# Reading the streamed operands of both feed-forward products from the last column to the first

## The chip, the cores and the metric

The kernel runs on one core of a Trainium2 chip. The metric is the device time of one execution in microseconds, of which the median of several runs is compared. Five engines matter: TensorE (PE in the profile, with its weight loads as PEld), VectorE (DVE), ScalarE (ACT), GpSimd (POOL) and SyncE (SP), whose queue carries the DMA transfers.

## The reference

The reference first runs a recurrence over 768 tokens for 4 batches of 8 heads of 48 channels, and then a feed-forward layer over all 3072 tokens, all in float32:

```python
for t in range(S):
    ar, ai = a_re_n[:, :, t, :, None], a_im_n[:, :, t, :, None]
    new_re = ar * S_re - ai * S_im
    new_im = ar * S_im + ai * S_re
    S_re, S_im = new_re + einsum('bhd,bhe->bhde', k[:, :, t], v[:, :, t]), new_im
    y[:, :, t] = einsum('bhd,bhde->bhe', q[:, :, t], S_re)
x = y.transpose(0, 2, 1, 3).reshape(3072, 384)
h = x @ w_in                       # 384 -> 2048
g = np.maximum(0.01 * h, h)
out = g @ w_out                    # 2048 -> 384
```

## The kernel before, in words

The recurrence is turned into attention over chunks of 128 tokens. For each of 12 units (a chunk of tokens of two batches) VectorE and ScalarE prepare decay factors, small tiled matmuls on TensorE make scores, values and the carried state, and the result, with channels on the 128 partitions and tokens along the columns, goes to a tile `x` of two halves: `xh` is the value rounded to float32r, written by ScalarE (`rounded`), and `xl` the remainder, written by VectorE (`rest`).

The feed-forward layer runs in 12 groups of 256 tokens (`GT`), one per unit. Each group goes through 8 steps of two blocks (`NF`) of 128 hidden channels. In a step, `first(g, s)` (line 1144) multiplies three 128-row blocks of `x` by the weights, which are split in two float32r parts like the data: hi by hi, lo by hi and hi by lo, so 9 matmuls a block and 18 a step, into one PSUM bank `ph`. `hide(g, s)` (line 1157) applies the leaky maximum with one ScalarE and one VectorE operation, and splits the result into `gh` and `gl`, the two halves of a tile `hid`, with one more of each. `second(g, s)` (line 1172) multiplies these by the second weights into three PSUM regions `po`, again 18 matmuls a step. In each of these matmuls the weights are the stationary operand (`lhsT`, 128 by 128) and the data are the streamed one (`rhs`, 128 rows of 256 columns that lie side by side in SBUF). Over 12 groups and 8 steps that is 12 * 8 * 36 = 3456 product matmuls. `store(g)` (line 1195) scales `po` on ScalarE and sends it out by DMA.

Columns are tokens, and no column of a product depends on another column of the data: matmul column j of `ph` is made of column j of `x`, and column j of `po` of column j of `hid`.

The order of the work is written by a planner. Every engine has a `Lane` (line 112), whose wrapper records each call with an estimated cost and chains it to the call before it on the same engine; `drive` (line 253) picks, each time, the task that can start earliest by those estimates, with ranks to break ties. For TensorE the estimate (`pe_costs`, line 157) is taken from the output's size, the kind of tile and the type of `lhsT`. `stream` (line 1205) fixes the order of first and second products inside a group, the second lagging three steps behind the first, and attention work of the next unit is placed between them.

In the attention part the scores (`scores`, line 940) read their streamed operand through `from_block` (line 914): of every four columns that lie side by side it takes the last 4, 3, 2 or 1, so a streamed row has 128, 96, 64 or 32 columns, always spread over the same 128 places of 4 bytes. In the profile these are the matmuls `att<-t` with 96x128, 96x96, 96x64 and 96x32. They are plain float32 matmuls, as are those named `att<-v,kn` and `att<-v,more`, which stream 48 columns side by side, and `att<-t,rst`, which streams 128 side by side.

All calls go through the wrapper on line 121, so the profile shows that line for nearly everything, and the groups are told apart by their tiles.

Of the kernel before, what the change touches and what calls it, by code (L numbers as in the profile page):

```python
# [26 lines left out]
NFC = DFF // P  # L27
NOC = DM // P
TI = 3
# [65 lines left out]
def block_lane(h, x):  # L95
    return (x + h) % NB


def score_order():

    todo = [[(h, x) for h in range(NB) for x in range(NB) if block_lane(h, x) == q] for q in range(NB)]
    free = [0] * NB
    order = []
    while any(todo):
        q = min((f, q) for q, f in enumerate(free) if todo[q])[1]
        h, x = todo[q].pop(0)
        order.append((h, x))
        free[q] += NB - x
    return order


class Lane:
# [343 lines left out]
def body(ctx, tc, keep, a_in, qk_in, v_in, w_in, out):  # L456
# [8 lines left out]
    win_hi = cp.tile([P, TI, DFF], F32R, tag="win_hi", name="win_hi")  # L465
    win_lo = cp.tile([P, TI, DFF], F32R, tag="win_lo", name="win_lo")
    wout_hi = cp.tile([P, NFC, DM], F32R, tag="wout_hi", name="wout_hi")
    wout_lo = cp.tile([P, NFC, DM], F32R, tag="wout_lo", name="wout_lo")
# [16 lines left out]
    mm = pe.matmul  # L485
# [434 lines left out]
    def xgroup(u):  # L920
        g = u // NGU
        if g not in xg:
            x = pp.tile([P, 2, TI, GT], F32R, tag="x", name=f"x_{g}", bufs=2)
            xg[g] = [x[:, 0], x[:, 1]]
        return *xg[g], (u % NGU) * C
# [3 lines left out]
    def attend(n):  # L929
# [10 lines left out]
        def scores(bi, hh):  # L940
            t96 = relay[n][1]
            ps[bi, hh] = bank = banks.take()
            for h4, x in score_order():
                h = hh * 4 + h4
                q = block_lane(h4, x)
                mm(
                    bank[32 * q : 32 * q + 32, h4].rearrange("p (y x) -> p y x", x=NB)[:, :, x:],
                    lhsT=from_block(t96, 1, h, bi, x, x + 1),
                    rhs=from_block(t96, 0, h, bi, x, NB),
                    start=True,  # L950
                    stop=True,
                )
# [35 lines left out]
        def values(bi):  # L988
            b = bs[bi]
            t96 = relay[n][1]  # L990
            v = raw_v[n]
            lanes4 = [[] for _ in range(4)]
            for x in range(4 * TI):
                k, part = divmod(x, 3)
                for h, off in ([(2 * k, 0)], [(2 * k, 32), (2 * k + 1, 48)], [(2 * k + 1, 80)])[part]:
                    cols = slice(k * PAIR + off, k * PAIR + off + 32)
                    first = off != 48
                    last = off != 32
                    lanes4[x % 4].append(
                        (x // 4, v[:, bi, cols], am[bi, h // 4][:, h % 4], first, last and c == 0)  # L1000
                    )
                    if c > 0:
                        lanes4[x % 4].append(
                            (x // 4, rst[:, b, k, off : off + 32], t96[:, slot_of(0, h), bi, 0:C], False, last)
                        )
            for step in zip(*lanes4):
                for q, (i, lhsT, rhs, first, last) in enumerate(step):
                    mm(px[bi][32 * q : 32 * q + 32, i], lhsT=lhsT, rhs=rhs, start=first, stop=last)
# [135 lines left out]
    def first(g, s):  # L1144
        xh, xl, _ = xgroup(g * GT // C)
        shown[g, s] = ph = psh.tile([P, NF, GT], F32, tag="h", name=f"ph_{g}_{s}")
        for x in range(NF):
            if x:
                yield "+P"
            fs = slice((s * NF + x) * P, (s * NF + x + 1) * P)  # L1150
            for k in range(TI):
                mm(ph[:, x], lhsT=win_hi[:, k, fs], rhs=xh[:, k], start=(k == 0), stop=False)
                mm(ph[:, x], lhsT=win_lo[:, k, fs], rhs=xh[:, k], start=False, stop=False)
            for k in range(TI):
                mm(ph[:, x], lhsT=win_hi[:, k, fs], rhs=xl[:, k], start=False, stop=(k == TI - 1))

    def hide(g, s):
        yield "A", *(freed(HID[s]) if g == 0 and s < 3 else [])
# [13 lines left out]
    def second(g, s):  # L1172
        if s == 0:
            both = [pso.tile([P, 512], F32, tag=f"o{o}", name=f"po_{g}_{o}") for o in range(2)]
            outs[g] = [both[o // 2][:, o % 2 * GT : o % 2 * GT + GT] for o in range(NOC)]
        po = outs[g]
        gh, gl = hid.pop((g, s))
        for x in range(NF):
            if x:
                yield "+P"  # L1180
            f = s * NF + x
            for o in range(NOC):
                os = slice(o * P, (o + 1) * P)
                share = dict(skip_group_check=True) if o < 2 else {}
                mm(po[o], lhsT=wout_hi[:, f, os], rhs=gh[:, x], start=(f == 0 and o != 1), stop=False, **share)
                mm(po[o], lhsT=wout_lo[:, f, os], rhs=gh[:, x], start=False, stop=False, **share)
        yield "+P"
        for x in range(NF):
            f = s * NF + x
            for o in range(NOC):  # L1190
                os = slice(o * P, (o + 1) * P)
                share = dict(skip_group_check=True) if o < 2 else {}
                mm(po[o], lhsT=wout_hi[:, f, os], rhs=gl[:, x], start=False, stop=(f == NFC - 1), **share)

    def store(g):
        yield "A", *([stored[g - 1]] if g else freed(STG))
# [8 lines left out]
    def stream(g):  # L1205

        late = [(second, g - 1, s) for s in (NS - 2, NS - 1)] if g - 1 in OVERLAP else []
        order = [(first, g, 0), *late, (first, g, 1), (first, g, 2)]
        for s in range(3, NS):
            order += [(second, g, s - 3), (first, g, s)]  # L1210
        order += [(second, g, NS - 3)]
        if g not in OVERLAP:
            order += [(second, g, s) for s in (NS - 2, NS - 1)]
        return order
# [139 lines left out]
```

## Time and profile before

| | |
|---|---|
| time, median of 3 runs | 601.63 us |
| the three runs | 598.35, 601.63, 604.72 us |
| the profiled execution, whole | 599.82 us |
| its span, first to last instruction | 598.1 us |
| mean granted TensorE clock, share of full | 0.979 |
| TensorE busy | 551.6 us, 92% |
| VectorE busy | 522.6 us, 87% |
| ScalarE busy | 388.4 us, 65% |

The profile is of one execution. Busy time is the time in which at least one instruction of an engine runs; TensorE's matmuls overlap one another, so the mean duration of one is longer than the distance from its start to the next one's start, and a group's busy time is less than its count times its mean. A stretch of back-to-back matmuls is read best from the chain of waits, which gives the time of so many in a row.

### The profile page before, as it was taken

How to read it: one execution, taken by the hardware profiler on the slowest of the kernel's cores; microseconds unless marked ns; L12 is line 12 of the kernel's file. 1: busy time of each engine (PE TensorE's matmuls, PEld its weight loads, DVE VectorE, ACT ScalarE, POOL GpSimd, SP SyncE). 2: the span in 40 equal slices, each digit the busy share in tenths (PEclk: the TensorE clock that was granted, in tenths of full speed). 3: DMA queues.
4: the chain of work that ended last, by engine and by line, in shares of the span. 5: the costliest groups of instructions: out<-in, count | busy, mean ns of one | idle time of the engine just before them, and what ended most of it. 6: DMA issues, size and time to landing. Idle time of an engine off the chain costs nothing.

```text
span 598.1 us, 17875 instructions
## 1 busy us (share of the span) xinstructions
PE 551.6 (92%) x7650; PEld 522.3 (87%) x7650; DVE 522.6 (87%) x897; ACT 388.4 (65%) x862; POOL 5.0 (1%) x23
## 2 busy tenths in 40 slices
PE   3865699999979899999999999999999999998996
PEld 2433499989969899999999999999999998998996
DVE  5999989999989999889999999999999998764232
ACT  7988586475474584584583674764755756775975
POOL 2000000000000000000000000000000000000000
PEclk9895799999999999999999999999999999999999
DMA  8973612522522423234235125125134266356650
GB/s 347 391 234 95 203 59 55 161 85 55 169 76 63 153 83 109 108 106 133 99 101 159 61 80 161 61 82 160 59 95 147 66 175 182 124 157 214 216 180 29
DMA packets 28370, 79.18 MB, mean 132 GB/s; under 512 B 3200, under 2 KB 9344, under 8 KB 28288
## 3 DMA queue, kind: packets, MB, share of 16 engines
q1 hardware_dynamic: 28288, 78.02, 41.1%
q8 instruction: 60, 0.98, 0.7%
q14 instruction: 22, 0.18, 0.1%
HBM read 54.26 MB, written 4.72 MB: 99 GB/s over the span
## 4 chain that ended last, share of the span: by engine, by line
PE 58%; DVE 20%; ACT 11%; DMA 7%; issue 3%; SPq 0%; DVEq 0%; ACTq 0%
PE po L121 21%; PE ph L121 20%; PE att L121 15%; DVE qkt L121 5%; DVE a L121 4%; DMA wck<-in_w_dram 3%; ACT wck L121 3%; DVE tg L121 2%; DMA t<-qkt 2%; DVE u L121 2%; DVE hid L121 2%; ACT rst L121 2%; DVE sq L121 1%; PE pd L121 1%; ACT tg L121 1%
## 5 line engine op out<-in xcount | busy, mean ns | idle before, releaser
L121 PE MATMUL ph<-x,win_hi 128*128 128x256 f32 x1152 | 215.7, 279 | 5.3 <-DVE tg L121 2.0
L121 PE MATMUL po<-hid,wout_hi 128*128 128x256 f32 x1152 | 215.3, 280 | 0.0
L121 PEld LDWEIGHTS ph<-x,win_hi 128*128 128x128 f32 x1152 | 181.4, 188 | 6.9 <-DVE tg L121 2.4
L121 PEld LDWEIGHTS po<-hid,wout_hi 128*128 128x128 f32 x1152 | 180.7, 188 | 1.6 <-issue 0.4
L121 PE MATMUL ph<-x,win_lo 128*128 128x256 f32 x576 | 141.6, 278 | 0.0
L121 PE MATMUL po<-hid,wout_lo 128*128 128x256 f32 x576 | 137.3, 278 | 0.0
L121 PEld LDWEIGHTS po<-hid,wout_lo 128*128 128x128 f32 x576 | 108.5, 188 | 0.0
L121 PEld LDWEIGHTS ph<-x,win_lo 128*128 128x128 f32 x576 | 108.4, 188 | 0.0
L121 ACT CAST hid<-tg 128x512 fp32r<-128x512 f32 x96 | 59.2, 616 | 52.7 <-DVE tg L121 50.9
L121 DVE TENSOR_TENSOR tg<-ph,tg 128x512 f32<-128x512 f32 x96 | 66.0, 687 | 30.5 <-ACT tg L121 30.4
L121 ACT ACTIVATE tg<-ph 128x512 f32<-128x512 f32 x96 | 56.7, 591 | 39.2 <-PE ph L121 38.9
L121 DVE TENSOR_TENSOR hid<-tg,hid 128x512 fp32r<-128x512 f32 x96 | 66.1, 688 | 14.2 <-ACT hid L121 13.3
L121 DVE TENSOR_TENSOR u<-a 128x384 f32<-128x384 f32 x84 | 46.6, 555 | 1.7 <-ACT a L121 0.2
L121 DVE TENSOR_TENSOR qkt<-qk,a 128x768 f32<-128x768 f32 x48 | 44.4, 956 | 2.6 <-ACT qkt L121 2.6
L121 PE MATMUL att<-t 96*32 96x96 f32 (+3 forms) x1536 | 36.9, 254 | 4.1 <-DMA t<-qkt 3.9
L121 PEld LDWEIGHTS att<-t 96*32 96x32 f32 x1536 | 33.8, 145 | 7.7 <-DMA t<-qkt 4.6
L121 PE MATMUL att<-t,rst 96*32 96x128 f32 x640 | 34.4, 272 | 1.6 <-issue 1.6
L121 ACT ACTIVATE wck<-wck 128x1152 f32<-128x1152 f32 (+1 forms) x22 | 27.2, 1238 | 11.5 <-DMA wck<-in_w_dram 11.4
L121 PE MATMUL att<-asb,v 128*32 128x128 f32 x592 | 33.9, 274 | 0.3 <-issue 0.3
L121 ACT ACTIVATE rst<-rst,t 96x48 f32<-96x48 f32 x128 | 29.8, 321 | 4.6 <-DVE rst L121 4.4
L121 DVE TENSOR_TENSOR a<-u 128x192 f32<-128x192 f32 x84 | 29.9, 356 | 1.9
L121 ACT ACTIVATE sq<-a 128x1536 f32<-128x1536 f32 x12 | 17.9, 1495 | 15.4 <-DMA a<-in_a_dram 15.4
(161 smaller groups left out, 769.8 us busy)
## 6 DMA issues: line engine op xcount, KB each, us to landing
t<-qkt SPq DMA_DIRECT2D x48, 290.2 KB, 4.2
wck<-in_w_dram SPq DMA_DIRECT2D x10, 1152.0 KB, 5.7
v<-in_v_dram SPq DMA_DIRECT2D x12, 832.0 KB, 4.7
a<-in_a_dram SPq DMA_DIRECT2D x12, 768.0 KB, 4.6
qk<-in_qk_dram SPq DMA_DIRECT2D x12, 768.0 KB, 5.9
out_dram<-ot SPq DMA_DIRECT2D x12, 384.0 KB, 2.7
t<-qkt SPq DMA_DIRECT2D x24, 129.0 KB, 4.1
stage_st<-in_w_dram SPq DMA_DIRECT2D x3, 768.0 KB, 4.5
```

The lines of the kernel that those rows point to most:

```text
L121: x = getattr(self.engine, name)(*args, **kw)
```

## The change

A new function `reverse` takes the access pattern of a streamed operand (128 partitions, n columns at a step of 1) and gives the same columns from the last to the first: the start moves by n - 1 columns, and the step becomes -1. All six product matmuls in the code, three in `first` and three in `second`, read their `rhs` through it. The stationary operands and the outputs are as before. So `ph` holds its 256 columns in reversed order, `hide` works on them where they stand, and `second` reverses them once more, so that `po` and the output are in the old order.

In the built program all 3456 streamed operands have a step of -1 and start at their last column. Each engine has the same instructions in the same order, with the same waits, as before; the planner's estimate for a matmul does not look at the streamed operand's step. Beyond line 109 all line numbers are higher by 5.

```diff
--- before.py
+++ after.py
@@ -107,6 +107,11 @@
         order.append((h, x))
         free[q] += NB - x
     return order
+
+
+def reverse(x):
+    step, n = list(x.ap)[1]
+    return bass.AP(x.tensor, x.offset + (n - 1) * step, [list(x.ap[0]), [-step, n]])
 
 
 class Lane:
@@ -1149,10 +1154,10 @@
                 yield "+P"
             fs = slice((s * NF + x) * P, (s * NF + x + 1) * P)
             for k in range(TI):
-                mm(ph[:, x], lhsT=win_hi[:, k, fs], rhs=xh[:, k], start=(k == 0), stop=False)
-                mm(ph[:, x], lhsT=win_lo[:, k, fs], rhs=xh[:, k], start=False, stop=False)
+                mm(ph[:, x], lhsT=win_hi[:, k, fs], rhs=reverse(xh[:, k]), start=(k == 0), stop=False)
+                mm(ph[:, x], lhsT=win_lo[:, k, fs], rhs=reverse(xh[:, k]), start=False, stop=False)
             for k in range(TI):
-                mm(ph[:, x], lhsT=win_hi[:, k, fs], rhs=xl[:, k], start=False, stop=(k == TI - 1))
+                mm(ph[:, x], lhsT=win_hi[:, k, fs], rhs=reverse(xl[:, k]), start=False, stop=(k == TI - 1))
 
     def hide(g, s):
         yield "A", *(freed(HID[s]) if g == 0 and s < 3 else [])
@@ -1182,15 +1187,15 @@
             for o in range(NOC):
                 os = slice(o * P, (o + 1) * P)
                 share = dict(skip_group_check=True) if o < 2 else {}
-                mm(po[o], lhsT=wout_hi[:, f, os], rhs=gh[:, x], start=(f == 0 and o != 1), stop=False, **share)
-                mm(po[o], lhsT=wout_lo[:, f, os], rhs=gh[:, x], start=False, stop=False, **share)
+                mm(po[o], lhsT=wout_hi[:, f, os], rhs=reverse(gh[:, x]), start=(f == 0 and o != 1), stop=False, **share)
+                mm(po[o], lhsT=wout_lo[:, f, os], rhs=reverse(gh[:, x]), start=False, stop=False, **share)
         yield "+P"
         for x in range(NF):
             f = s * NF + x
             for o in range(NOC):
                 os = slice(o * P, (o + 1) * P)
                 share = dict(skip_group_check=True) if o < 2 else {}
-                mm(po[o], lhsT=wout_hi[:, f, os], rhs=gl[:, x], start=False, stop=(f == NFC - 1), **share)
+                mm(po[o], lhsT=wout_hi[:, f, os], rhs=reverse(gl[:, x]), start=False, stop=(f == NFC - 1), **share)
 
     def store(g):
         yield "A", *([stored[g - 1]] if g else freed(STG))
```

## Rows read from the trace of the kernel before

**Rows 1.** The page: span, engines, the last chain by engine and line.

```profile
span 598.1 us, 17875 instructions
...
PE 551.6 (92%) x7650; PEld 522.3 (87%) x7650; DVE 522.6 (87%) x897; ACT 388.4 (65%) x862; POOL 5.0 (1%) x23
...
PE 58%; DVE 20%; ACT 11%; DMA 7%; issue 3%; SPq 0%; DVEq 0%; ACTq 0%
PE po L121 21%; PE ph L121 20%; PE att L121 15%; DVE qkt L121 5%; DVE a L121 4%; DMA wck<-in_w_dram 3%; ACT wck L121 3%; DVE tg L121 2%; DMA t<-qkt 2%; DVE u L121 2%; DVE hid L121 2%; ACT rst L121 2%; DVE sq L121 1%; PE pd L121 1%; ACT tg L121 1%
```

**Rows 2.** Three windows of all engines, in us: busy, instructions, clock, DMA.

```profile
core 0: us, PE busy (x) PEld busy (x) DVE busy (x) ACT busy (x) POOL busy (x), PEclk, DMA share, GB/s
0.00:76.00 76.00, 46.96 (x321) 27.01 (x321) 68.64 (x114) 60.21 (x113) 3.80 (x13) 0.84 0.71 250
76.00:592.00 516.00, 503.43 (x7320) 494.32 (x7321) 452.54 (x768) 326.35 (x745) 1.20 (x10) 1.00 0.38 116
592.00:598.10 6.10, 1.24 (x11) 0.93 (x10) 1.36 (x16) 1.81 (x6) 0.00 (x0) 0.85 0.20 69
```

**Rows 3.** The page: product matmuls, busy us and mean ns, idle before.

```profile
L121 PE MATMUL ph<-x,win_hi 128*128 128x256 f32 x1152 | 215.7, 279 | 5.3 <-DVE tg L121 2.0
L121 PE MATMUL po<-hid,wout_hi 128*128 128x256 f32 x1152 | 215.3, 280 | 0.0
...
L121 PE MATMUL ph<-x,win_lo 128*128 128x256 f32 x576 | 141.6, 278 | 0.0
L121 PE MATMUL po<-hid,wout_lo 128*128 128x256 f32 x576 | 137.3, 278 | 0.0
```

**Rows 4.** Chain of waits, stretch 254 to 280: start us, us, what.

```profile
254.31 2.04 PE ph L121 x18
256.35 2.04 PE po L121 x18
...
264.51 4.08 PE ph L121 x36
...
276.75 2.04 PE po L121 x18
```

**Rows 5.** Chain of waits, stretch 296 to 340, same columns.

```profile
296.93 2.12 PE ph L121 x18
299.05 2.12 PE po L121 x18
...
307.53 4.24 PE ph L121 x36
...
322.37 2.12 PE ph L121 x18
...
325.19 2.75 PE att L121 x90
```

**Rows 6.** Windows, the matmuls into ph alone, four stretches.

```profile
core 0: us, PE busy (x), PEclk, DMA share, GB/s
81.00:113.00 32.00, 15.92 (x126) 1.00 0.34 92
212.00:240.00 28.00, 13.54 (x108) 1.00 0.37 104
296.00:325.00 29.00, 15.82 (x126) 1.00 0.39 103
552.00:593.00 41.00, 18.10 (x144) 1.00 0.44 145
```

**Rows 7.** Windows, the matmuls into po alone, the same four stretches.

```profile
81.00:113.00 32.00, 15.11 (x120) 1.00 0.34 92
212.00:240.00 28.00, 14.51 (x114) 1.00 0.37 104
296.00:325.00 29.00, 15.14 (x120) 1.00 0.39 103
552.00:593.00 41.00, 24.68 (x198) 1.00 0.44 145
```

**Rows 8.** Groups by shape, attention matmuls, stretch 325 to 346.

```profile
L121 PE MATMUL att<-t,rst 96*32 96x128 f32 x64 | 3.4, 272 | 0.0
...
L121 PE MATMUL att<-t 96*32 96x128 f32 x32 | 2.8, 274 | 0.0
L121 PE MATMUL att<-t 96*32 96x96 f32 x32 | 2.8, 249 | 0.0
L121 PE MATMUL att<-t 96*32 96x32 f32 x32 | 2.8, 237 | 0.0
L121 PE MATMUL att<-t 96*32 96x64 f32 x32 | 2.8, 240 | 0.0
...
L121 PE MATMUL att<-v,more 128*32 128x48 f32 x48 | 0.9, 206 | 0.0
```

## The prediction

> **What bounds the kernel now.** I read the page first. TensorE is busy for 92% of the 598.1 us span and VectorE for 87%, and the chain that ended last lies on TensorE for 58%, the two products alone taking 41% [rows 1]. [...]
>
> The third view is the table of groups: 1152 + 1152 + 576 + 576 = 3456 product matmuls with a mean of 278 to 280 ns [rows 3]. That mean is the length of one matmul from start to modelled end, and neighbours overlap, so it is not what one costs. The chain of waits gives that: 18 matmuls in a row take 2.04 us in one stretch, 2.04/18 = **113.3 ns** each, and 36 take 4.08 [rows 4]; in another, 18 take 2.12 us, **117.8 ns** each [rows 5]. A stretch has one pace from end to end, for `ph` and `po` alike, and the paces change only where attention work broke the stream; they do not go with a buffer or a product. The slower pace holds in four stretches, with 126 + 108 + 126 + 144 = 504 matmuls into `ph` [rows 6] and 120 + 114 + 120 + 198 = 552 into `po` [rows 7], in all 1056 of 3456. I have no cause for it in the rows.
>
> **The change, part by part.**
>
> *What is added or removed.* No instruction, no wait and no transfer; the order on each engine stays. The count of product matmuls stays at 3456 with 256 columns each, weights and outputs are untouched, and `hide` works on columns in place, so ScalarE and VectorE read and write what they did, where they did. Those terms are 0, and they need no cover, since there is no work to hide.
>
> *The streamed read at a step of -1.* This is the only term: 3456 times an unknown x, the extra distance from one matmul's start to the next. No row of the trace shows a negative step, so I bound x by the nearest rows, the scores of attention, which read with gaps [rows 8]. A row of 128 columns side by side takes 272 ns and one of 48 takes 206, so a column costs (272 - 206)/80 = 0.825 ns in these float32 matmuls. By that line 32 columns side by side would take 206 - 16 * 0.825 = 193 ns, 64 would take 219, and 96 would take 246. The scores' rows of 32, 64 and 96 columns, which are one, two and three out of every four, take 237, 240 and 249: excesses of 44, 21 and 3 ns. With four out of four, 274 against 272, it is 2. So the cost is not that of a step that differs from 1 as such; it goes with how little of each four neighbouring columns (16 bytes) is used. Walking backwards uses all four, one after the other, and 256 columns from a start at the last column cover the same 64 fours as before. So the row nearest to the changed read is the one with four of four, and I take **x = 0**.
>
> The upper bound is that every column costs what it costs when it is alone in its four: 44/32 = 1.375 ns a column, 256 * 1.375 = 352 ns a matmul, 3456 * 0.352 = 1217 us. A middle one is that only each new four is late, 64 * 1.375 = 88 ns a matmul, 304 us. On the lower side, a gain from the read itself is bounded by the two paces: all matmuls at 113.3 ns would give back 1056 * 4.44 ns = 4.7 us. [...]
>
> [...]
>
> *The sum.* 599.82 us for the profiled execution plus 0. That execution lies 1.8 us under the median of 601.63, and the runs shown spread from 598.35 to 604.72; with no change the new median should come out near both, and I say **601 us**.
>
> **The rivals.**
>
> *A late line (slower).* The place is the read of `rhs` in all 3456 matmuls. If what feeds the array fetches ahead only in rising order, or keeps no line when the address falls, each new four arrives late, or each column fetches its four again. Against it: the scores show a cost for wasted columns and nearly none for a gap as such (3 ns at three of four). For it: there is no slack. The lone-column form takes 32 * 0.825 + 44 = 70 ns for 32 fours, 2.2 ns each, while a product at 113.3 ns takes a four every 1.77 ns already; the float32 matmuls, at 0.825 ns a column, ask for half as much as the products do, so they cannot show that a backward walk is fed fast enough. The prices are those above: 904 us when only the fours are late, up to 1817 us when each column is. [...] Chance **0.15**.
>
> *The slower pace everywhere.* If the pace depends on how the streamed read falls against something else in the machine, reading from the other end could put all stretches at 117.8 ns: (3456 - 1056) * 4.44 ns = 10.7 us, 610.5 us. For it: two paces exist, and something sets them. Against it: within one kernel, with the same buffers and addresses in turn, both occur. Chance **0.06**.
>
> *The faster pace everywhere.* 599.8 - 4.7 = 595.1 us, for the same reasons the other way round. Chance **0.05**.
>
> *The change does not do what it says.* The operands in the built program have a step of -1 and start at the last column, so it is in; if a later layer ordered the columns again, the time would be that of no cost. It has no share of its own.
>
> **How the numbers follow.** No cost holds 1 - 0.15 - 0.06 - 0.05 = **0.74** and gives 601 us; how many stretches fall into which pace shifts it by a few us from run to run, about as far as the runs shown spread, so its own range is 596 to 607. The range for 8 times in 10 adds both pace cases, 594 to 612, and holds about 0.74 + 0.06 + 0.05 = 0.85 less what strays; the late line stays outside it, because its prices lie hundreds of microseconds off and would make the range say nothing. About 1%, or 6 us, is what a measurement of this kernel can tell from no change. Faster by over 1% needs a time under 595.6, which the faster pace gives, narrowly, most of the time: 0.05 with what strays from the likeliest case. Slower by over 1%, over 607.6: 0.15 + 0.06 and 0.01 that strays, **0.22**. Within 1%: **0.73**.
>
> **What would show it.** In the chain of waits after, stretches of 18 product matmuls should again take 2.04 or 2.12 us, a stretch keeping one pace; the groups of product matmuls should keep means near 276 to 282 ns, and the window from 76 to 592 us its length. With a late line, 18 matmuls would take 3.6 us (113.3 + 88 ns each) to 8.4 us, the means would grow by the same amount each, the weight loads between them would wait, and VectorE and ScalarE would idle on `ph` where VectorE now is busy for 452.54 of 516 us. If only one pace is left in all stretches, the pace rivals are right. What would make the prediction wrong is a price of the backward step that the scores, which only ever walk upwards, cannot show; a small one, of 2 to 5 ns a matmul, would end at the upper edge of the range, and looks like the slower pace until the numbers of columns tell them apart.

## The result and the profile after

The changed kernel takes 608.09 us (median of 12 runs, 605.98 to 611.58), the kernel before 601.59 us over 12 runs of its own. The ratio is 1.0107 with a 95% interval of 1.0075 to 1.0139: slower, by 1%, where no change was forecast. The profiled execution took 606.89 us, 7.07 us more than the one before.

The page of the changed kernel, with its span, the engines, the last chain by engine, and the four groups of product matmuls:

```profile
span 605.2 us, 17875 instructions
...
PE 559.6 (92%) x7650; PEld 530.7 (88%) x7650; DVE 523.7 (87%) x897; ACT 389.3 (64%) x862; POOL 5.0 (1%) x23
...
PE 61%; DVE 28%; ACT 5%; issue 4%; DMA 2%; DVEq 0%; SPq 0%; ACTq 0%
...
L126 PE MATMUL ph<-x,win_hi 128*128 128x256 f32 x1152 | 220.9, 283 | 5.2 <-DVE x L126 2.1
L126 PE MATMUL po<-hid,wout_hi 128*128 128x256 f32 x1152 | 220.2, 283 | 0.0
...
L126 PE MATMUL ph<-x,win_lo 128*128 128x256 f32 x576 | 144.5, 281 | 0.0
L126 PE MATMUL po<-hid,wout_lo 128*128 128x256 f32 x576 | 140.4, 281 | 0.0
```

The span is 7.1 us longer than in [rows 1]. The means of the product matmuls rose from 278 to 280 ns [rows 3] to 281 to 283, by 3 to 4 ns; VectorE's and ScalarE's busy times rose by about 1 us. So little is added in each of very many matmuls. The chain of waits tells how much (start us, us, what):

```profile
254.89 2.12 PE ph L126 x18
257.01 2.12 PE po L126 x18
...
265.49 4.24 PE ph L126 x36
...
298.42 2.12 PE ph L126 x18
300.54 2.12 PE po L126 x18
...
326.69 2.74 PE att L126 x87
```

Every long stretch now reads 2.12 us for 18, or 4.24 for 36: 117.8 ns from one matmul to the next; the single distances, from the timeline, go 115, 118, 120 in turn. (In the slow stretches of the kernel before they are 117, 118 and 119: the same mean, but not the same pattern.) The stretch near 260 us was at 113.3 ns before [rows 4], the one near 300 us at 117.8 already [rows 5]; in the changed kernel no long stretch at 113.3 ns is left. The starts in the timeline add up the same way: the distances under 130 ns between neighbouring product matmuls sum to 386.7 us before (3365 of them) and to 396.4 after (3364), **9.7 us more**.

Not all of that reached the end. The window that holds the products is 523 us long now and was 516 [rows 2]:

```profile
core 0: us, PE busy (x) PEld busy (x) DVE busy (x) ACT busy (x) POOL busy (x), PEclk, DMA share, GB/s
...
76.00:599.00 523.00, 511.92 (x7320) 503.56 (x7321) 454.40 (x769) 327.55 (x745) 1.20 (x10) 1.00 0.37 114
```

TensorE is busy 8.5 us longer in it and idle 11.1 us where it was idle 516.00 - 503.43 = 12.6. The place is seen in the chain between 128 and 153 us, by line, of the kernel before and then of the changed one:

```profile
by line: DVE a L121 26.3%; DVE qkt L121 21.2%; DVE tg L121 16.8%; DVE hid L121 14.2%; DVE u L121 9.8%; issue 6.0%; DVE sq L121 3.5%; DVE qk L121 2.9%; DVE sm L121 0.4%; DVEq L121 0.2%; DVE pt L121 0.2%
```

```profile
by line: DVE qkt L126 28.2%; DVE a L126 26.4%; DVE tg L126 16.8%; DVE hid L126 14.0%; DVE u L126 9.9%; issue 6.2%; DVE sq L126 3.5%; DVE qk L126 2.9%; DVE sm L126 0.4%; DVEq L126 0.2%; DVE pt L126 0.2%
```

In that stretch, and on to about 193 us, VectorE ends last in both kernels, so slower products cost next to nothing there: the long stretch of products that starts at 177.15 us before starts at 177.47 after, though most of some 300 matmuls between 125 and 177 us had gone from 113.3 to 117.8 ns. Later, where the chain lies mostly on TensorE, the delay grows from stretch to stretch: 253.56 to 254.14, 339.51 to 341.19, 424.01 to 428.20, 506.67 to 512.38, 552.73 to 559.67 us.

### The profile page after: what moved, and what is told of

Same layout as the page of the kernel before. It is cut to its first block, busy times and chain, and to the rows that moved or that the text cites. A ratio compares the mean times of both kernels' runs of the same rounds, so it can differ in the third digit from the quotient of the medians.

```text
span 605.2 us, 17875 instructions
## 1 busy us (share of the span) xinstructions
PE 559.6 (92%) x7650; PEld 530.7 (88%) x7650; DVE 523.7 (87%) x897; ACT 389.3 (64%) x862; POOL 5.0 (1%) x23
## 4 chain that ended last, share of the span: by engine, by line
PE 61%; DVE 28%; ACT 5%; issue 4%; DMA 2%; DVEq 0%; SPq 0%; ACTq 0%
PE ph L126 24%; PE po L126 23%; PE att L126 13%; DVE a L126 6%; DVE qkt L126 5%; DVE u L126 4%; DVE tg L126 2%; DVE hid L126 2%; DVE sq L126 2%; ACT rst L126 1%; PE pd L126 1%; DVE xs L126 1%; DMA t<-qkt 1%; DVE asb L126 1%; DVE stage_st L126 1%
## 5 line engine op out<-in xcount | busy, mean ns | idle before, releaser
L126 PE MATMUL ph<-x,win_hi 128*128 128x256 f32 x1152 | 220.9, 283 | 5.2 <-DVE x L126 2.1
L126 PE MATMUL po<-hid,wout_hi 128*128 128x256 f32 x1152 | 220.2, 283 | 0.0
L126 PE MATMUL ph<-x,win_lo 128*128 128x256 f32 x576 | 144.5, 281 | 0.0
L126 PE MATMUL po<-hid,wout_lo 128*128 128x256 f32 x576 | 140.4, 281 | 0.0
L126 PE MATMUL att<-t 96*32 96x64 f32 (+3 forms) x1536 | 35.1, 252 | 1.9 <-DMA t<-qkt 1.9
```

The lines of the kernel that those rows point to most:

```text
L126: x = getattr(self.engine, name)(*args, **kw)
```

## The experiments

The theories: **A**, each backward matmul pays a fixed few ns at its hand-over to the next; **B**, each four of columns costs more backwards, in proportion to their number; **C**, the direction costs nothing and the pace comes from elsewhere (chance, or other engines). A later one, **D**, is stated where it arose.

### TensorE alone, sixteen forms of matmul (bench)

```python
for r in range(ROUNDS):
    for name, x0, n, step, wstep, ostep in FORMS:
        ...
        fill(FILL[(r + at) % len(FILL)])
        ...
        for i in range(COUNT):
            pe(
                span(t, 0, n, ostep), lhsT=span(w, (i % 15) * P, P, wstep), rhs=span(x, x0 + 256 * (i // 2 % 3), n, step),
                start=(i == 0), stop=(i == COUNT - 1),
            )
```

There are 6 rounds, COUNT is 36, and `fill` issues the 5 to 20 small matmuls between bursts. The kernel leaves out all of the reference's computation and writes zeros.

> Not the reference's computation: TensorE alone runs bursts of 36 back-to-back float32r matmuls of one form each, every one with other weights, six bursts a form, with 5 to 20 small matmuls between bursts. Forms: 256 columns upwards and downwards, outputs written downwards, weights at a step of 2, a start one column off, a step of +2 and -2, and 128, 240, 288 and 512 columns in both directions. Theory A (a backward read costs each matmul a fixed few ns at its hand-over, and a forward one sometimes escapes it): the 256-column bursts downwards all at 117.8 ns, upwards some at 113.3 and some at 117.8; at 512 columns both directions near 213 to 220 ns, with the same 0 to 5 ns between them. Theory B (each new four of columns costs more backwards, 4.4 ns over 64 fours): 2.2 ns more at 128 columns and 9 ns more at 512. Theory C (nothing in TensorE tells the directions apart, and the pace comes from traffic of other engines): all 256-column bursts at one pace in both directions.

The chain of waits, one round: start us, us, form, 36 matmuls each. A burst's time holds its first matmuls, which are uneven; the distances given below it are start to start over the last 15 of a burst, from the timeline, and the six bursts of a form agree to 0.6 ns, save those at a step of +2, which spread over 3.5 ns, and one downward burst of 240 columns.

```profile
15.95 4.50 PE up L51 x36
...
21.23 4.46 PE down L51 x36
...
48.42 8.34 PE uptwo L51 x36
...
57.55 8.58 PE downtwo L51 x36
...
67.13 4.17 PE upshort L51 x36
...
72.50 4.17 PE downshort L51 x36
...
77.90 8.39 PE uplong L51 x36
...
86.84 8.60 PE downlong L51 x36
...
96.02 4.23 PE upmid L51 x36
...
101.03 4.22 PE downmid L51 x36
```

- 512 columns: 226.7 ns upwards, 233.3 downwards. That is 113.3 and 116.7 for each 256. Theory C falls: the chain of waits names TensorE alone from 14.88 to 125 us, and the directions differ.
- 128 and 240 columns: 111.4 to 112.1 ns in both directions (one downward burst at 113.3). Nearly twice the columns cost no more, so at these two lengths something else sets the pace, and the direction does not show. Each of these matmuls loads 128 weight columns, and I take the load to be what sets it, which is an estimate: no form with fewer weight columns was run at these lengths.
- A step of +2 or -2 over 256 columns takes 227 to 230 and 233 ns, about as long as 512 columns side by side. This fits a price by the fours of columns (16 bytes, at 4 bytes a column) that are passed, 128 in both cases, and not by columns. A step of 4, which would pass twice as many, was not run.
- 256 columns: 119.9 to 120.0 ns upwards, 118.1 to 118.5 downwards. Here the forward read is the slower, and no burst reached 113.3 ns. No theory expected that.
- 288 columns: 131.5 to 132.1 ns upwards, 133.3 downwards. In proportion to 512 columns the forward read would take 288/512 of 226.7, or 127.5 ns, so it is 4 to 4.6 ns slower than that here.
- 256 columns upwards with the output written downwards, or with the weights at a step of 2: 119.9 to 120.1 ns, as without.

Theory B expected 9 ns between the directions at 512 and 2.2 at 128, A up to 5 ns at 512, with both directions near 213 to 220 ns, a pace that no run shows; measured were 6.7, between 226.7 and 233.3, and 0. From this came theory **D**, a guess from these numbers: a matmul's pace is the slower of loading weights (for 128 of them I take the 111.6 ns that 128 and 240 columns took) and streaming (113.3 or about 117 ns for 256, half of what 512 took), and where the two are close they hold each other up, at 113 to 120 ns.

### The kernel before, once more (before_again)

No line is changed.

> The kernel before, once more, for a second draw of its paces. If the pace of a stretch is settled by chance where the stream starts anew, the stretches at 117.8 ns lie elsewhere than in the first profile (which had them at 81 to 113, 212 to 240, 296 to 325 and 552 to 593 us). If it is settled by addresses or by the program, they lie at the same places.

598.40 us. In the chain of waits, two of the stretches shown in [rows 4, 5]:

```profile
254.44 2.12 PE ph L121 x18
256.56 2.12 PE po L121 x18
...
297.89 2.04 PE ph L121 x18
299.93 2.04 PE po L121 x18
```

The paces have changed places: 117.8 ns near 260 us and 113.3 near 300, where the first profile had it the other way round. The last stretch, from 552 us, was at 117.8 and is at 113.4 now; the one from 82 us is at 117.8 in both. So in the forward kernel the pace of a stretch differs from one execution to the next, and is not a property of its addresses or its place in the program alone. I call it a draw below; what settles it is not shown.

### The first product alone, the second alone (first_only, second_only)

```diff
-mm(po[o], lhsT=wout_hi[:, f, os], rhs=reverse(gh[:, x]), ...
+mm(po[o], lhsT=wout_hi[:, f, os], rhs=gh[:, x], ...
...
```

That is first_only, with the other two matmuls of the second product alike; second_only undoes the three of the first product in the same way.

> Only the first product reads backwards; the output's columns then stand in reversed order within each group of 256. Theory A: inside one stretch the matmuls into ph run at 117.8 ns, and those into po at 113.3 or 117.8, so 602 to 608 us. If the pace belongs to the whole stretch and is settled at its start, ph and po share a pace in every stretch, and since the stretches begin with po the time is that of before, 598 to 605 us.

> Only the second product reads backwards; the output's columns stand in reversed order within each group of 256. Theory A: po at 117.8 ns, ph at 113.3 or 117.8, 602 to 608 us, as with the first product alone. If a stretch has one pace, settled where it starts, all stretches that begin with po are at 117.8 ns and the time is that of the changed kernel, 606 to 611 us.

First only: 605.97 us, ratio 1.0059 (1.0027 to 1.0092). Second only: 605.08 us, ratio 1.0058 (1.0021 to 1.0095). Each half costs 0.6%, and the two together come to about the 1.07% of the whole. The times alone decide little against the rival, one pace for a whole stretch: first only lies 1 us above its 598 to 605 us, second only 0.9 us below its 606 to 611. The distances decide. The chains of waits of one stretch, first only and then second only:

```profile
342.96 2.12 PE ph L126 x18
345.08 2.05 PE po L126 x18
347.13 2.12 PE ph L126 x18
349.25 4.09 PE po L126 x36
```

```profile
342.69 2.05 PE ph L126 x18
344.74 2.12 PE po L126 x18
346.86 2.05 PE ph L126 x18
348.92 4.24 PE po L126 x36
```

Within one stretch the product that reads backwards runs at 2.12/18 = 117.8 ns and the other at 2.05/18 = 113.9, which holds the first three or four distances after each border, at 115 to 120 ns, and 113.3 after them. So the slower pace of a backward product is not settled at a stretch's start, as I had read [rows 4, 5]; it goes with the matmul's own read. Over the whole run the backward product has a mean distance of 117.8 ns in both (breaks aside), and the upward one 114.3 and 114.5.

The forward product does not follow its own read alone. Of its 136 blocks of 18 or more in these two runs 132 settle at 113.3 ns; the other four run at 117.8 throughout. In the kernel before a pace, once there, lasts until the stream is next broken, as from 254.31 to 278.79 us [rows 4] and from 296.93 to 324.49 [rows 5]. So 117.8 ns has two sources: the backward read has it in every block of these two runs, with single distances near 115, 118 and 120 ns, and the forward read has it at times, mostly with 117, 118 and 119, for a cause that no run here shows.

### TensorE alone, the order of fours against the order inside (bench2)

```python
if kind == "up":
    dims, first = [[1, n]], 0
elif kind == "down":
    dims, first = [[-1, n]], n - 1
elif kind == "turn":
    dims, first = [[block, n // block], [-1, block]], block - 1
else:
    dims, first = [[-block, n // block], [1, block]], n - block
```

The last branch is the form called back. This kernel, too, computes nothing of the reference.

> Not the reference's computation: TensorE alone, bursts of 36 float32r matmuls in the order of weights and data that the first product has, six bursts a form, small matmuls between. Forms: 256 columns with 128 weight columns, 256 with 64 weight columns (half), 512 with 128 (long); each up, down, turn (groups of four columns rising, the four inside falling) and back (groups of four falling, the four inside rising); and at 512 groups of 16 columns, turn and back. In the first measurement 512 columns took 226.7 ns upwards and 233.3 downwards, and 128 or 240 columns took 111.6 in both directions, so theory D: a matmul's pace is the slower of loading the next weights (111.6 ns for 128 columns) and streaming, streaming costs 226.7/512 = 0.443 ns a column upwards and 0.456 downwards, and 256 columns stand where the two meet. Theory D expects half up at 113.3 and half down at 116.7 ns in every burst, with no lottery, and 256 with 128 weight columns above these, 113 to 120. Its rival, a fixed cost of each backward matmul (theory A), expects half up and half down 4.4 to 6.7 ns apart, as at 512. Where theory D holds: if the falling order of the fours costs, long turn is 226.7 and long back 233.3; if the falling order inside a four costs, turn is 233.3 and back 226.7; if both are needed, both are 226.7. The groups of 16 tell whether the unit is four columns or more: the same as with groups of four if it is four.

The chain of waits, one round, 36 matmuls each:

```profile
146.13 4.24 PE halfup L56 x36
...
151.37 4.39 PE halfdown L56 x36
...
156.96 4.25 PE halfturn L56 x36
...
162.44 4.38 PE halfback L56 x36
...
167.38 8.38 PE longup L56 x36
...
176.34 8.60 PE longdown L56 x36
...
185.72 8.39 PE longturn L56 x36
...
195.11 8.60 PE longback L56 x36
...
204.92 9.79 PE longsix L56 x36
...
215.94 8.60 PE longsixback L56 x36
```

Steady distances, from the timeline, the six bursts of a form within 0.1 ns of one another:

| form | up | turn | back | down |
|---|---|---|---|---|
| 256 columns, 64 weight columns | 113.3 | 113.3 | 117.8 | 117.8 |
| 512 columns, 128 weight columns | 226.7 | 226.7 | 233.3 | 233.3 |

Turn equals up and back equals down: with groups of four, the falling order of the fours is what costs, and a step of -1 inside them is free. With half the weights to load, the forward read of 256 columns is at 113.3 ns in all six bursts and the backward one at 117.8: the means of both paces of the kernel, without any draw. So 117.8 ns is what streaming 256 columns backwards took with 64 weight columns, and 113.3 what it took forwards. With all 128 weight columns the forward read was at 120.0 ns again (the first burst aside, where the granted clock was 0.53), and turn too, and down and back at 118.0 to 118.5. The kernel's forward pace of 113.3 ns with 128 weight columns was not seen in either bench. Theory D had 116.7 for half down, from half of 233.3; that is 1.1 ns short. Theory A's 4.4 to 6.7 ns was met there, but not its fixed cost: the price is 4.4 at 256 and 6.7 at 512, neither fixed nor in proportion.

The groups of 16 columns were expected to do as the groups of four, and one of the two did not. Groups falling with the columns rising inside took 233.3 ns, the same as for fours, though only one in four of the steps from a four to the next falls there. Groups rising with the columns falling inside took 266.7 ns where 226.7 was expected: three in four of those steps fall, with a jump ahead after every fourth, and the order costs 40 ns and not 6.7. So the price does not go by the number of falling steps, and what happens at one of them stays open.

### Fours rising, columns inside falling, in the kernel (turn); the other half (back)

```diff
 def reverse(x):
     step, n = list(x.ap)[1]
-    return bass.AP(x.tensor, x.offset + (n - 1) * step, [list(x.ap[0]), [-step, n]])
+    return bass.AP(x.tensor, x.offset + 3 * step, [list(x.ap[0]), [4 * step, n // 4], [-step, 4]])
```

The outputs of the six matmuls get the matching shape, 64 by 4. For back the offset is `(n - 4) * step` and the dimensions are `[-4 * step, n // 4], [step, 4]`.

> Both products read their fours of columns in rising order and the four columns inside falling, so every column still changes its place and the step inside is -1; the output is in the old order. The bench says that this streams as fast as the forward read (113.3 ns for 256 columns where the weights don't hold it up, 226.7 for 512). If the falling order of the fours is the cause in the kernel too, stretches at 113.3 ns are back beside stretches at 117.8, and the time is that of the kernel before, 598 to 605 us. If any negative step, or the pattern with two dimensions, is what costs, all stretches stay at 117.8 to 120 ns and the time at 606 us or more.

> The other half: both products read the fours in falling order and the four columns inside rising, with a step of +1 inside. By the bench it streams like the whole backward read (117.8 ns and 233.3). If the order of the fours is the cause, no stretch runs at 113.3 ns and the time is that of the changed kernel, 606 to 611 us; if the step inside is, 598 to 605 us.

Turn: 602.63 us, ratio 1.0035 (1.0010 to 1.0061). Back: 607.85 us, ratio 1.0135 (1.0099 to 1.0171). The chains of waits, turn and then back:

```profile
256.84 2.12 PE ph L130 x18
258.96 2.12 PE po L130 x18
...
300.28 2.04 PE ph L130 x18
302.32 2.04 PE po L130 x18
```

```profile
254.54 2.12 PE ph L130 x18
256.66 2.12 PE po L130 x18
...
298.02 2.12 PE ph L130 x18
300.14 2.12 PE po L130 x18
```

Turn has both paces again: four of its twelve long stretches run at 117.8 ns, as many as in the first profile before, and its distances under 130 ns sum to 385.4 us, where that profile had 386.7. Back has no stretch at 113.3 ns, and one at a third pace, 120.0 ns, that no other profile of the whole kernel shows:

```profile
472.16 2.16 PE ph L130 x18
474.32 2.16 PE po L130 x18
```

Turn's time lies 0.35% above before's, and its interval does not reach 1. With the breaks counted its products take 402.9 us against 401.7, 1.2 of the 3.25 us between the two profiled executions; the rest lies outside the products, and I have no reason for it.

## Why the prediction was wrong, by its own steps

- **The step that failed is x = 0.** I had it from the scores: all four of each four columns are used, so the cost is that of four of four. The inference left out the order in which the fours come. Every row of [rows 8] walks them upwards; the runs show that walking them downwards takes 117.8 ns for 256 columns in place of 113.3, so x is 4.4 ns for a matmul that was at 113.3 and 0 for one that was at 117.8 already. The rows were also means of single durations, while x is a distance between starts; [rows 8] give all four forms of the scores the same busy time, 2.8 us for 32 of each.
- **The late line**, a line being a four of columns, named the right place, the order of the fours, and missed the size by 20 times: spread over the fours the price is 4.4/64 = 0.07 ns each, not 1.375. Even that is only an average, since the groups of 16 show that the price does not go by falling steps. It came from rows in which most of a four is wasted, which is another cost. Whether anything fetches ahead, or keeps a four, as it supposed, no run shows. The argument for it, that a product takes a four every 1.77 ns with no slack, was sound: with 64 weight columns the forward read takes the same 113.3/64.
- **The slower pace everywhere**, at a chance of 0.06, is what the profile shows: 117.8 ns in every long stretch. I counted 3456 - 1056 = 2400 matmuls at 4.44 ns, 10.7 us; 9.7 us came. Of the 3365 distances under 130 ns in the first profile 1184 were at 115.5 ns or more, and the other 2181 at 4.44 ns are 9.7 us. I gave it little because both paces occurred in one kernel and I had no cause. The cause turned out to be the direction: after the change no long stretch was at 113.3 ns. That this rival's 610.5 us came within 2.4 us of the median is partly luck, since it named no mechanism.
- **The whole price on the path.** The sum of that rival, 599.8 + 10.7 us, puts all that the matmuls lose on the time, which was too strong: of 9.7 us 7.1 reached the span. TensorE's idle time between 76 and 592 us, 516.00 - 503.43 = 12.6 us [rows 2], was not the only cover: between about 128 and 193 us VectorE ends last, and the slower products before 177 us delayed the stretch that starts there by 0.3 us.
- **What the forecast had right:** the busy times of the other engines moved by about 1 us, and the time lies within 594 to 612 us. It does so because that range was widened for the rivals of pace; it lies above the 596 to 607 us of the likeliest case, no cost.

The cause is shown in the order of the fours (bench2, turn, back) and in its place in the kernel (first only, second only). Why falling fours cost what they do, and what decides a forward stretch's draw between 113.3 and 117.8 ns, stay open. A version with 512 columns a matmul, in which the forward read took 226.7 ns in every burst, was not tried: its outputs need three PSUM tiles of 512 columns where the kernel has two.

## What to carry to other kernels

Price a changed access pattern by the order in which it passes fours of columns, not only by how many it uses: here the same 64 fours, with 64 weight columns, took 113.3 ns rising and 117.8 falling. At 128 and 240 columns, where something else set the pace (111.4 to 112.1 ns), the direction cost nothing; at 256 in this kernel there was no slack to hide even 4 ns, and over 3456 matmuls 9.7 us came together. If columns may be taken in another order, turning them inside fours and leaving the fours rising streamed as fast as the plain read, 113.3 ns for 256 columns with 64 weight columns and 226.7 for 512. And where two paces appear in one trace, take a second profile before calling them a property of the program.

## What the runs showed of the hardware

- Float32r streaming in bursts: 256 columns (64 fours of 16 bytes, 64 weight columns) took 113.3 ns rising and 117.8 falling, 512 columns (128 fours, 128 weight columns) 226.7 and 233.3, and 256 columns at a step of 2 (also 128 fours and 128 weight columns) 227 to 230 upwards and 233.3 downwards.
- A matmul that loads 128 weight columns did not repeat faster than 111.4 ns, whether it streamed 128 or 240 columns.
- With 256 columns and 128 weight columns the forward read took 120.0 ns in the bench and 113.3 or 117.8 in the kernel, the backward read 118.0 to 118.5 in the bench and 117.8 in the kernel, or 120.0 in one stretch of back.
- A start one column off its four took 123.3 to 123.5 ns for 256 columns upwards and 120.0 downwards.
